# Attention with squared relu and an MLP behind it on one core: how the fourth and fifth head unit get transposed, and the order of the first loads

## The chip, the cores and the metric

The kernel runs on one core of one Trainium2 chip. The metric is the device time of one execution in microseconds (us); less is better. Before the change it is 379.6 us, the median of three runs (379.3 to 379.73).

## What is computed

```
scores = q @ k.T / sqrt(64)                  # 8 batches, 12 heads, 448 positions, head size 64
attn   = max(scores, 0)**2 / 448
x      = attn @ v                            # heads side by side: 3584 rows of 768
h      = x @ w_in                            # 768 -> 2048
out    = max(h, 0)**2 @ w_out                # 2048 -> 768
```

All inputs and the output are float32 in HBM; inside the kernel the operands are float16, which the loads make of them.

## The kernel before, in words

**Units and tiles.** Four heads of one batch are a *unit*: three units per batch, 24 in all, numbered 0 to 23. A unit has seven *tiles* (J = 7) of 64 key positions for each of its heads, so tile t belongs to unit t // 7; unit 4 begins with tile 28, unit 5 with 35, unit 6 with 42. For its scores a unit needs q and k with the head dimension on the partitions, that is transposed (`qT`, `kT`, from a pool of three buffers).

**Two ways to the transpose.** Units 0 to 5 (NPE = 6) are loaded by `load16` (lines 93 and 94: one DMA of 224 KB for q, one for k, in pieces of 896 B) and transposed on PE by `pe_transpose` (28 transposes into PSUM, line 222, and two copies out of it, lines 214 on ACT and 216 on DVE). Units 6 to 23 are loaded by `load_qk` (line 108: four DMAs of 112 KB, in pieces of 128 B, two for q and two for k) into `qs` and `ks`, and transposed by `dma_transpose`: two DMA transposes that SP issues (line 119), each after both halves of its source have landed. `load_v` (line 99) loads a unit's v, `load_w1` (line 134) a quarter of w_in in two DMAs, `load_w2` (line 140) a quarter of w_out.

**Queues.** All loads are issued by POOL, in the order of the program; at most eight are under way, since POOL waits for the eighth last before it issues the next. SP issues DMA transposes and stores. Each engine takes its instructions in the order in which the program writes them.

**The first part (up to about 26 us).** Batch 0, units 0 to 2, has nothing to lie beside: `visit` makes two tiles of scores (line 252, each twice, to keep PE busy), ACT applies the relu (line 256), DVE squares (line 369), and `av_some` multiplies attn with v (line 270) two visits later. PE transposes units 1, 2 and 3 in visits 1, 4 and 10.

**The h pass of batch 0 and 1 (about 28 to 84 us).** `h_group(b, f)` makes one block of 128 hidden units: six matmuls (line 420), relu on ACT or DVE, square on DVE. Between the blocks lies the attention of batch 1, units 3 to 5: an event list gives each piece of it a time on a clock that counts h matmuls (T_G = 6 x 0.1892 us a block, T_H = 16 blocks). `visit` now makes two tiles of scores, and `av_unit` a whole unit's attn x v (28 matmuls, line 317) once its seven tiles are there. In the second half of this pass, which belongs to batch 1, the events bring differences of w_out's quarters (`sums_w2`, DVE, line 151) and of w_in's (`sums_w1`), and the DMA transposes of units 6 and 7. Tile 42, the first of unit 6, comes at T_H + 8 T_G.

**The rest.** The out pass of batches 0 and 1 (line 729) and then, batch pair by batch pair, the h pass in a seven-product form (line 550) and the out pass, with the attention of the following pair between the blocks. What DVE may do late is kept in queues that a planner empties: it adds up the time of PE (`at_pe`) and of DVE (`at_ve`) from costs written in the code, 2.65 us for an `av_unit` and 0.19 + 0.38 per tile for a visit, and puts a piece of DVE work where it expects DVE to be free.

**PSUM.** Scores and transposes share the pool `slot` (two buffers of two banks, and a third one, `third`, up to its close). The h blocks' pool `mma` takes the banks of `third`; `mmb` those of the two pools of attn x v of batch 0 (`rounds`).

Around the change, the order of the first loads before it is:

```
load16(0); load_v(0); load16(1); load_v(1); load16(2); load_v(2)
# in visit 0: load16(3); load_w1(0); load_w1(1); load_v(3)
# in visit 2: load16(4); load_w1(2); load_v(4)
# in visit 5: load16(5); load_w1(3); load_v(5)
load_v(6); load_w2 (b11, b12, b22, b21); load_qk(6); load_qk(7)
```

Of the kernel before, what the change touches and what calls it, by code (L numbers as in the profile page):

```python
# [12 lines left out]
AF = mybir.ActivationFunctionType  # L13
# [4 lines left out]
def kernel(  # L18
# [9 lines left out]
    nc = tc.nc  # L28
# [13 lines left out]
    P = 128  # L42
    J = 7
# [4 lines left out]
    NF = FF // P  # L48
# [21 lines left out]
    PSUM = bass.MemoryType.PSUM  # L70
# [19 lines left out]
    def load16(n):  # L90
        tq = q16_p.tile([P, 2, J * D], FP16, name="q16", tag="q16")
        tk = q16_p.tile([P, 2, J * D], FP16, name="k16", tag="k16")
        nc.gpsimd.dma_start(out=tq, in_=heads(q, n))
        nc.gpsimd.dma_start(out=tk, in_=heads(k, n))
        q16s[n] = (tq, tk)

    def load_v(n):
        t = v_p.tile([P, 2, J * D], FP16, name="vt", tag="vt")
        nc.gpsimd.dma_start(out=t, in_=heads(v, n))
        vts[n] = t  # L100

    def load_qk(n):

        blks[n] = []
        for src, nm in ((q, "qs"), (k, "ks")):
            t = blk_p.tile([P, J, 2, D], FP16, name=nm, tag=nm)
            for hh in range(2):
                nc.gpsimd.dma_start(  # L108
                    out=t[:, :, hh, :],
                    in_=heads(src, n)[:, hh].rearrange("p (j d) -> p j d", d=D))  # L110
            blks[n].append(t)
# [20 lines left out]
    def load_w1(i):  # L132
        for hh in range(2):
            nc.gpsimd.dma_start(
                out=w1[i][64 * hh:64 * hh + 64],
                in_=moe_w_in[:, 512 * i:512 * (i + 1)].rearrange(
                    "(hh m d) f -> hh d m f", hh=2, d=D)[hh])
# [7 lines left out]
    def sums_w2(i):  # L145


        op, c = divmod(i, 2)
        c = slice(4 * c, 4 * c + 4)
        dst, x, y = ((t1, b12, b11), (t3, b22, b12), (t2, b22, t1), (nt4, b21, t2))[op]  # L150
        nc.vector.tensor_sub(dst[:, c], x[:, c], y[:, c])
# [5 lines left out]
    nc.vector.memset(zeros, 0.0)  # L157
    junk = const_p.tile([P, 1], FP16, name="junk", tag="junk")
    nc.scalar.activation(out=junk, in_=zeros[:, 0:1], func=AF.Relu)
    load_v(0)  # L160
    load16(1)
    load_v(1)
    load16(2)
    load_v(2)

    def sums_w1(i):

# [38 lines left out]
    def pe_transpose(n):  # L206
        srcs = q16s.pop(n)
        ts = new_qkt()
        ps = slot(FP16)

        def copy(i, eng):
            dst = ts[i].rearrange("p j c -> p (j c)")
            if eng == 0:
                nc.scalar.activation(out=dst, in_=pss[i][:, i, 0:J * P], func=AF.Copy)  # L214
            else:
                nc.vector.tensor_copy(dst, pss[i][:, i, 0:J * P])

        pss = [ps, slot(FP16) if n == 0 else ps]
        for i, src in enumerate(srcs):
            for j in range(J):  # L220
                for hh in range(2):
                    nc.tensor.transpose(  # L222
                        pss[i][64 * hh:64 * hh + 64, i, j * P:(j + 1) * P],
                        src[:, hh, j * D:(j + 1) * D], ident)
            if n == 0:
                copy(i, 1)
                warm(1)
        qkt[n] = ts
        if n == 3:
            return lambda: (copy(0, 0), copy(1, 0))  # L230
        if n > 0:
            copy(0, n < 3)
            copy(1, n < 3)
        return None


    xts: dict = {}
# [63 lines left out]
    def av_unit():  # L301

        n = unit[0]
        if n == NUN or seen.get(n * J + J - 1, 10 ** 6) >= now[0]:
            return
        unit[0] += 1
        flush(rest=False)
        at_pe[0] += 2.65
        b, u = divmod(n, NU)
        vt = vts[n]  # L310
        ps = slot(FP32)
        for j in range(J):
            at = ats.pop(n * J + j)
            for hp in range(2):
                r = slice(64 * hp, 64 * hp + 64)
                for hh in range(2):
                    nc.tensor.matmul(  # L317
                        ps[64 * hh:64 * hh + 64, hp, 0:S],
                        lhsT=vt[r, hh, j * D:(j + 1) * D], rhs=at[r, hh, :],
                        start=(j == 0), stop=(j == J - 1))  # L320
        if u == 0:
            xts[b] = x_p.tile([P, NM, S], FP16, name="xt", tag="xt")
        nc.scalar.activation(
            out=xts[b][:, 2 * u:2 * u + 2, :], in_=ps[:, :, 0:S],
            func=AF.Copy, scale=CX)
# [16 lines left out]
    at_pe = [0.0]  # L342
# [28 lines left out]
    def visit(tiles, turn=None, lag=2, most=3):  # L371
        now[0] += 1
        for t in tiles:
            if t % J == 0 and t >= NPE * J:
                prefetch(t // J + 2)
        if big:
            for t in tiles[:1]:
                score(t)
            av_unit()
            for t in tiles[1:]:  # L380
                score(t)
            at_pe[0] += 0.19 + 0.38 * len(tiles)
            for i, t in enumerate(tiles):
                square(ats[t], 0.6 + 0.85 * i)
            return
        for t in tiles:
            score(t, 2)
        later = pe_transpose(turn) if turn is not None else None
        flush()
        av_some(lag, most)  # L390
        if later:
            later()
        for t in tiles:
            square(ats[t])
        flush()
# [16 lines left out]
    def h_group(b, f):  # L412
        z = (b % 2) * S
        cell = [None]

        def step(m):
            def run():
                if m == 0:
                    cell[0] = mm_tile()
                nc.tensor.matmul(  # L420
                    cell[0][:, 0:S],
                    lhsT=w1[f // 4][:, m, (f % 4) * P:(f % 4 + 1) * P],
                    rhs=xts[b][:, m, :], start=(m == 0), stop=(m == NM - 1))
                if m < NM - 1:
                    return
                f0 = f - f % 2
                g = g_of(b)[:, f0:f0 + 2, z:z + S]
                if b == 0 and (f % 2 == 1 or f == 0) and f < 14:
                    nc.vector.tensor_scalar(
                        out=g[:, f % 2], in0=cell[0][:, 0:S],  # L430
                        scalar1=0.0, scalar2=None, op0=ALU.max)
                else:
                    nc.scalar.activation(
                        out=g[:, f % 2], in_=cell[0][:, 0:S], func=AF.Relu)
                flush()
                if b == 0 and f == NF - 1:
                    square(g)
                elif f % 2 == 1:
                    nc.vector.tensor_mul(g, g, g)
            return run  # L440

        return [(0.1892, step(m), m == 0) for m in range(NM)]
# [330 lines left out]
    NB0 = NU * J  # L773
    warm(10)
    pe_transpose(0)
    for i in range(11):
        visit([t for t in (2 * i, 2 * i + 1) if t < NB0],
              turn={1: 1, 4: 2, 10: 3}.get(i))
        if i == 0:
            load16(3)  # L780
            load_w1(0)
            load_w1(1)
            load_v(3)
        if i == 2:
            load16(4)
            load_w1(2)
            load_v(4)
        if i == 5:
            load16(5)
            load_w1(3)  # L790
            load_v(5)
    load_v(6)
    load_w2(b11, 0, 0)
    load_w2(b12, 0, 1)
# [2 lines left out]
    load_qk(6)  # L797
    load_qk(7)
    first.close()
    big.append(ctx.enter_context(tc.tile_pool(name="mma", bufs=2, space=PSUM)))  # L800


    f0 = h_group(0, 0)
    for _, fn, _ in f0[0:4]:
        fn()
    av_some(0, 9)
    rounds.close()
    big.append(ctx.enter_context(tc.tile_pool(
        name="mmb", bufs=2, space=PSUM, side="right", reuse_waits="tile")))
    visit([NB0, NB0 + 1])  # L810

    T_G = NM * 0.1892
# [3 lines left out]
    begin = [sum(T_O[:pr]) + 2 * (T_H + T_S * (pr - 1)) * (pr > 0) for pr in range(B // 2)]  # L816

    events = []
    seq = [[2, 3], 4, [4, 5], [6, 7], [8, 9], 5, [10, 11], [12, 13], [14, 15],
           [16, 17], [18, 19], [20], []]  # L820
    for i, ts in enumerate(seq):
        at = (2.5 + i) * T_G
        if isinstance(ts, int):
            events.append((at, lambda n=ts: pe_transpose(n)))
        else:
            events.append((at, lambda ts=ts: visit([NB0 + t for t in ts])))

    def ready():
        early.close()
# [3 lines left out]

    events.append((T_H + 0.2, ready))
    for i in range(8):
        events.append((T_H + (1 + i // 2) * T_G, lambda i=i: sums_w2(i)))
    for i in range(6):
        events.append((T_H + (8 + i) * T_G, lambda i=i: sums_w1(i)))
    for i in range(2):
        events.append((2 * T_H + 3 + 3 * i, lambda i=i: sums_w1(6 + i)))  # L840
    for m in (6, 7):
# [33 lines left out]
    for i in (1, 2):  # L875
        events.append((2 * T_H - (3 - i) * T_G, lambda i=i: outs[0][1](i)))

    steps = [(0.1892, None, False)] * 4 + f0[4:]
    for f in range(1, NF):
        steps += h_group(0, f)  # L880
    for f in range(NF):
        steps += h_group(1, f)
# [49 lines left out]
```

## Time and profile before

| what | us |
|---|---|
| median of three runs | 379.6 |
| the profiled execution, its own time | 379.35 |
| its span, first to last instruction | 377.6 |
| PE busy | 363.5 (96%) |
| DVE, ACT, POOL busy | 278.6, 249.8, 107.1 |
| PE idle from 0 to 8, 8 to 30 and 30 to 60.7 us | 1.7, 3.1, 1.1 |
| PE idle from 60.7 to 84.4 us | 0.0 |
| PE idle from 371 us to the end | 5.1 |
| one DMA transpose, from issue to landing (median) | 4.5 (qT), 4.2 (kT) |
| one load_qk half, one load_v, from issue to landing (median) | 4.4 to 5.3, 6.6 |

The page gives, for each engine, the busy time and its share of the span; then the span in 40 slices, with the busy share of each in tenths; the DMA queues (q0 is POOL's loads, q1 is SP's transposes and stores); and the groups of instructions by line, with tile names as out<-in. A wait is put down to what came last. The chain of waits is followed back from the last instruction, and the engine with most of it sets the end: here PE has 81%. The time from issue to landing of a DMA contains the time that it stands behind earlier ones in its queue.

### The profile page before, as it was taken

Reading aid. Unit: us, or ns where it says so; the run is one execution under the profiler, and the core shown is the slowest. Engines: PE = TensorE matmul, PEld = TensorE weight load, DVE = VectorE, ACT = ScalarE, POOL = GpSimd, SP = SyncE. Lnnn points to the kernel's source line nnn. Section 1 sums busy time; section 2 is a strip of 40 time slices with the busy share of each in tenths; the row PEclk is TensorE's granted clock in tenths of the full one; section 3 lists DMA queues with packets and bytes.
Section 4 is the critical chain, followed back from the end, with each engine's and each line's share of the span. In section 5 each row is a group of like instructions: output and inputs, shape, how many; then the busy total and the mean of one; then the engine's idle time right before and its main releaser. Section 6 shows DMA issues by size and latency. Waiting matters only on the chain.

```text
span 377.6 us, 8806 instructions
## 1 busy us (share of the span) xinstructions
PE 363.5 (96%) x3600; PEld 231.3 (61%) x3600; DVE 278.6 (74%) x515; ACT 249.8 (66%) x373; POOL 107.1 (28%) x128
## 2 busy tenths in 40 slices
PE   7889999999999999999999999999999999999994
PEld 3544444444455678785555577877555588985663
DVE  1796567997767689897965758989956688995542
ACT  2897996686677798775566578877766785532220
POOL 8545431944440444404042243150000000000001
PEclk9999999999999999999999999999999999999998
DMA  8999999999999999789498997893132200002333
GB/s 120 197 204 205 205 203 177 124 171 134 121 139 187 134 114 139 90 95 82 96 112 134 184 178 68 83 110 63 38 97 69 76 26 2 2 0 65 94 96 84
DMA packets 121160, 42.65 MB, mean 113 GB/s; under 512 B 100832, under 2 KB 117760, under 8 KB 121120
## 3 DMA queue, kind: packets, MB, share of 16 engines
q0 software_dynamic: 82912, 23.01, 59.9%
q1 hardware_dynamic: 38048, 18.98, 26.2%
q8 instruction: 28, 0.46, 0.5%
q10 hardware_dynamic: 160, 0.10, 0.1%
q14 instruction: 12, 0.10, 0.1%
HBM read 45.61 MB, written 11.01 MB: 150 GB/s over the span
## 4 chain that ended last, share of the span: by engine, by line
PE 81%; ACT 6%; DVE 6%; issue 2%; DMA 2%; POOL 1%; POOLq 0%; ACTq 0%; DVEq 0%
PE mm L729 33%; PE mm L550 23%; PE slot L252 9%; PE mm L420 9%; PE slot L317 7%; ACT at L256 4%; DVE at L369 2%; DMA k<-in_k_dram 2%; PE slot L222 1%; DVE g L491 1%; ACT m L486 1%; DVE xt L283 1%; DVE s L602 1%; DVE g L498 0%; ACT qT L214 0%
## 5 line engine op out<-in xcount | busy, mean ns | idle before, releaser
L256 ACT ACTIVATE at<-slot 128x896 f16<-128x896 f32 x168 | 146.2, 920 | 33.0 <-PE slot L252 33.0
L369 DVE TENSOR_TENSOR at<-at 128x896 f16<-128x896 f16 x168 | 99.7, 618 | 15.7 <-ACT at L256 14.5
L108 POOL DMA_DIRECT2D qs<-in_q_dram x36 | 35.4, 984 | 121.3 <-DMA qT<-qs 113.6
L729 PEld LDWEIGHTS <-s 128*128 128x128 f16 x440 | 41.7, 98 | 32.0 <-issue 4.3
L252 PE MATMUL slot<-qT,kT 64*64 64x448 f16 x756 | 58.1, 360 | 2.6 <-ACT at L256 1.2
L550 PEld LDWEIGHTS <-w 128*128 128x128 f16 x576 | 54.4, 98 | 5.9 <-issue 5.4
L550 PE MATMUL mm<-xt,w 128*128 128x224 f16 x432 | 48.6, 259 | 0.0
L729 PEld LDWEIGHTS <-g 128*128 128x128 f16 x336 | 31.5, 98 | 24.0 <-issue 5.0
L550 PEld LDWEIGHTS <-ws 128*128 128x128 f16 x432 | 40.2, 98 | 6.7 <-issue 6.7
L729 PE MATMUL mm<-b,g 128*128 128x384 f16 x224 | 40.7, 326 | 0.0
L420 PE MATMUL mm<-xt,w 128*128 128x448 f16 x192 | 39.6, 353 | 0.3 <-ACT xt L280 0.3
L729 PE MATMUL mm<-b,s 128*128 128x384 f16 x216 | 39.6, 326 | 0.1
L729 PE MATMUL mm<-t,s 128*128 128x384 f16 x224 | 39.5, 326 | 0.0
L636 DVE SCALAR_TENSOR_TENSOR osb<-mm,u 128x384 f32<-128x384 f32 (+1 forms) x30 | 16.2, 541 | 31.2 <-ACT u L631 23.0
L252 PEld LDWEIGHTS <-kT 64*64 64x64 f16 x756 | 19.9, 104 | 31.1 <-issue 25.7
L108 POOL DMA_DIRECT2D ks<-in_k_dram x36 | 35.0, 975 | 9.9 <-DMA b<-in_moe_w_out_dram 5.8
L631 ACT ACTIVATE u<-mm 128x384 f32<-128x384 f32 x28 | 13.7, 491 | 32.6 <-PE mm L729 31.4
L571 POOL DMA_DIRECT2D out_dram<-osb x2 | 1.1, 563 | 120.5 <-DVE osb L636 120.5
L550 PE MATMUL mm<-x,ws 128*128 128x224 f16 x288 | 34.4, 259 | 0.9 <-ACT m L486 0.9
L317 PE MATMUL slot<-at,vt 64*64 64x448 f16 x588 | 32.2, 350 | 0.6 <-DVE at L369 0.5
L498 DVE TENSOR_TENSOR g<-g 128x896 f16<-128x896 f16 x48 | 29.7, 619 | 1.1 <-ACT g L501 0.2
L420 PEld LDWEIGHTS <-w 128*128 128x128 f16 x192 | 17.3, 98 | 19.1 <-issue 4.8
(66 smaller groups left out, 400.2 us busy)
## 6 DMA issues: line engine op xcount, KB each, us to landing
out_dram<-osb SPq DMA_DIRECT2D x52, 192.0 KB, 3.3
vt<-in_v_dram POOLq DMA_DIRECT2D x24, 224.0 KB, 6.6
qs<-in_q_dram POOLq DMA_DIRECT2D x36, 112.0 KB, 4.4
ks<-in_k_dram POOLq DMA_DIRECT2D x36, 112.0 KB, 5.3
w<-in_moe_w_in_dram POOLq DMA_DIRECT2D x8, 384.0 KB, 11.5
b<-in_moe_w_out_dram POOLq DMA_DIRECT2D x4, 768.0 KB, 17.1
q<-in_q_dram POOLq DMA_DIRECT2D x6, 224.0 KB, 8.3
k<-in_k_dram POOLq DMA_DIRECT2D x6, 224.0 KB, 8.6
```

The lines of the kernel that those rows point to most:

```text
L108: nc.gpsimd.dma_start(out=t[:, :, hh, :], in_=heads(src, n)[:, hh].rearrange("p (j d) -> p j d", d=D))
L222: nc.tensor.transpose(pss[i][64 * hh:64 * hh + 64, i, j * P:(j + 1) * P], src[:, hh, j * D:(j + 1) * D], ident)
L252: nc.tensor.matmul(ps[c, hh, 0:S], lhsT=kT[r, j, c], rhs=qT[r, :, c], start=True, stop=True)
L256: nc.scalar.activation(out=at, in_=ps[:, :, 0:S], func=AF.Relu, scale=SK)
L317: nc.tensor.matmul(ps[64 * hh:64 * hh + 64, hp, 0:S], lhsT=vt[r, hh, j * D:(j + 1) * D], rhs=at[r, hh, :], start=(j == 0), stop=(j == J - 1))
L369: lambda: nc.vector.tensor_mul(at, at, at), 0))
L420: nc.tensor.matmul(cell[0][:, 0:S], lhsT=w1[f // 4][:, m, (f % 4) * P:(f % 4 + 1) * P], rhs=xts[b][:, m, :], start=(m == 0), stop=(m == NM ...
L498: due_g.append((t, 0.54, lambda: nc.vector.tensor_mul(g, g, g), b))
L550: nc.tensor.matmul(XY[s][y][:, r * Q:(r + 1) * Q], lhsT=left(k, i0 + 2 * s + r, m), rhs=right(k, m), start=(fresh and r == 0 and m == 0), ...
L631: nc.scalar.activation(out=t, in_=X[0][:, 0:HALF], func=AF.Copy, scale=CO)
L636: nc.vector.scalar_tensor_tensor(out=osb[row][:, c], in0=acc[0][:, 0:cc.stop - cc.start], scalar=CO, in1=keep[nm][:, cc], op0=ALU.mult, op ...
L729: nc.tensor.matmul(acc[0][:, 0:HALF], lhsT=left()[:, f], rhs=right[:, f], start=(fresh and f == 0), stop=(f == KH - 1), skip_group_check=n ...
```

## The change

Four things are changed.

- **Loads.** The q and k of units 1 and 2 are loaded ahead of the v of the unit before them. Unit 3 is loaded ahead of w_in. Units 4 and 5 are loaded by `load_qk`: unit 4 ahead of the first quarter of w_in, unit 5 ahead of v of unit 3 and the third quarter.
- **Transposes.** Units 4 and 5 go by `dma_transpose`, written after visit 6 and after the last visit of batch 0. `pe_transpose` of unit 3 comes after that visit's attn x v, and its kT is copied by DVE instead of ACT.
- **First h blocks.** Before, four matmuls of block 0 stood ahead of the last attn x v of batch 0. Now a part of attn x v stands ahead of the first two, and two more of block 0 and two of block 1 follow after the rest of it.
- **Events and costs.** The visits of batch 1 come every 1.33 blocks from 1.5 on. `sums_w2` and `sums_w1` come later. The planner's costs are 1.33 for an `av_unit` and 0.19 + 0.19 per tile for a visit.

PE loses 56 transposes and 56 weight loads by this, SP gains four DMA transposes; the bytes loaded are the same.

```diff
+    load16(1)
     load_v(0)
-    load16(1)
+    load16(2)
     load_v(1)
-    load16(2)
     load_v(2)
+    load16(3)
+    load_qk(4)
...
         if n == 3:
-            return lambda: (copy(0, 0), copy(1, 0))
+            return lambda: (copy(0, True), copy(1))
...
-        at_pe[0] += 2.65
+        at_pe[0] += 1.33
...
-            at_pe[0] += 0.19 + 0.38 * len(tiles)
+            at_pe[0] += 0.19 + 0.19 * len(tiles)
...
     for i in range(11):
-        visit([t for t in (2 * i, 2 * i + 1) if t < NB0],
-              turn={1: 1, 4: 2, 10: 3}.get(i))
+        visit([t for t in (2 * i, 2 * i + 1) if t < NB0], turn={1: 1, 4: 2}.get(i))
         if i == 0:
-            load16(3)
             load_w1(0)
             load_w1(1)
+        if i == 2:
+            load_qk(5)
             load_v(3)
-        if i == 2:
-            load16(4)
             load_w1(2)
             load_v(4)
         if i == 5:
-            load16(5)
             load_w1(3)
             load_v(5)
+        if i == 6:
+            dma_transpose(4)
+    later = pe_transpose(3)
+    dma_transpose(5)
     load_v(6)
...
-    big.append(ctx.enter_context(tc.tile_pool(name="mma", bufs=2, space=PSUM)))
-    f0 = h_group(0, 0)
-    for _, fn, _ in f0[0:4]:
-        fn()
+    big.append(ctx.enter_context(tc.tile_pool(
+        name="mma", bufs=2, space=PSUM, reuse_waits="tile")))
+    f0, f1 = h_group(0, 0), h_group(0, 1)
+    def some(part):
+        for _, fn, _ in part:
+            fn()
+    av_some(1, 9)
+    some(f0[0:2])
+    later()
     av_some(0, 9)
...
+    some(f0[2:4])
+    some(f1[0:2])
     visit([NB0, NB0 + 1])
...
-    seq = [[2, 3], 4, [4, 5], [6, 7], [8, 9], 5, [10, 11], [12, 13], [14, 15],
-           [16, 17], [18, 19], [20], []]
-    for i, ts in enumerate(seq):
-        at = (2.5 + i) * T_G
-        if isinstance(ts, int):
-            events.append((at, lambda n=ts: pe_transpose(n)))
-        else:
-            events.append((at, lambda ts=ts: visit([NB0 + t for t in ts])))
+    for i in range(11):
+        ts = [NB0 + t for t in (2 * i + 2, 2 * i + 3) if t < NB0]
+        events.append(((1.5 + 1.33 * i) * T_G, lambda ts=ts: visit(ts)))
...
     for i in range(8):
-        events.append((T_H + (1 + i // 2) * T_G, lambda i=i: sums_w2(i)))
+        events.append((T_H + (4 + 0.75 * i) * T_G, lambda i=i: sums_w2(i)))
     for i in range(6):
-        events.append((T_H + (8 + i) * T_G, lambda i=i: sums_w1(i)))
+        events.append((T_H + (10 + 0.8 * i) * T_G, lambda i=i: sums_w1(i)))
...
-    steps = [(0.1892, None, False)] * 4 + f0[4:]
-    for f in range(1, NF):
+    steps = [(0.1892, None, False)] * 6 + f1[2:4] + f0[4:6] + f1[4:6]
+    for f in range(2, NF):
```

## The prediction

> **What bounds the kernel now.** I read the page first (sections 1 and 2), then PE's waits up to 75 us, the chain of waits in order of time, SP's timeline, and last the DMA view stretch by stretch. TensorE (PE) is busy 96% of the span, so an edit pays only by taking PE work or PE waits away. PE's waits in the part that the change touches are few:
>
> ```profile
> PE slot L222 <- ACT at L256: 1.0, 3, 0.6
> PE slot L222 <- DMA k<-in_k_dram: 0.7, 1, 0.7
> PE avt L270 <- DVE xt L283: 0.7, 3, 0.4
> PE slot L252 <- ACT kT L214: 0.5, 2, 0.3
> ```
>
> The columns are total us, times, longest. The second line is k of unit 1 coming late; the fourth is the score blocks that wait for the PSUM copies of units 4 and 5. The chain shows the two PE transposes themselves, and the place where unit 6 is first used:
>
> ```profile
> 4.81 6.64 DMA k<-in_k_dram
> ...
> 34.78 0.92 PE slot L222 x28
> 35.72 0.92 ACT qT L214
> ...
> 44.25 0.92 PE slot L222 x28
> ...
> 60.80 10.32 PE mm L420 x54
> 71.12 0.50 PE slot L252 x8
> ```
>
> (start us, us). From 60.80 on PE runs without a gap, and at 71.12 it takes the first score tile of unit 6 (tile 42), the first unit that goes by DMA transposes. When these came is in SP's timeline:
>
> ```profile
> 59.98 1.31 SPq L119 DMA_TRANSPOSE qT<-qs  x1
> 61.55 1.23 SPq L119 DMA_TRANSPOSE kT<-ks  x1
> ```
>
> The second landed 4.4 us after its issue, at 61.55 + 4.4 = 65.95. SP issued it at once when the fourth load of unit 6 landed (issued on POOL at 42.95, 18.5 us to landing: 61.45). **So unit 6 has 71.12 - 65.95 = 5.17 us in hand, and that is all.** The last view is the DMA queues in four stretches (23 to 43 us; 57 to 61.5; 64 to 66; 72 to 81):
>
> ```profile
> DMA packets 4563, 4.09 MB, mean 204 GB/s; under 512 B 211, under 2 KB 4562, under 8 KB 4562
> ```
> ```profile
> DMA packets 5350, 0.70 MB, mean 156 GB/s; under 512 B 5308, under 2 KB 5350, under 8 KB 5350
> ```
> ```profile
> DMA packets 2176, 0.55 MB, mean 276 GB/s; under 512 B 2175, under 2 KB 2175, under 8 KB 2175
> ```
> ```profile
> q0 software_dynamic: 4397, 0.89, 123.0%
> q1 hardware_dynamic: 1856, 0.46, 52.0%
> ```
>
> The first is loads in the 896 B and 1 KB form (load16, load_v, load_w1): 204 GB/s. The second is load_qk's 128 B form alone: 156. The third is DMA transposes alone: 276. The fourth mixes loads (q0) and two transposes (q1). The DMA row of the page stands at 9 from the second slice to the sixteenth: from about 4 us until unit 6 and 7 have landed the loads leave no hole. There are thus two limits: PE, and 5 us behind it the DMA stream that ends with unit 6.
>
> [...]
>
> **The change part by part.** Sums are against the profiled execution: span 377.6 us, own time 379.35 (1.75 us around the span), 0.25 us under the median of 379.6.
>
> 1. k of unit 1 ahead of v0. The fourth load of the queue landed at 4.10 + 4.6 = 8.7 us, the fifth at 11.45. k1 becomes the fourth; its q is transposed at 10.20, held by ACT, so k no longer waits: -0.72 us. v0, now fifth, lands at about 11.45 and is first used at 12.79 - 0.72 = 12.07: hidden, 0.6 us to spare.
>
> 2. The last attn x v. Eight of its matmuls move ahead of unit 3's transposes and fill 0.50 of the 0.57 us in which these wait for ACT (at 26.57), and the four h matmuls that follow cover the copy to xt (0.25 us at 30.22, of which the rest of the new order keeps some): I take -0.55 us together. reuse_waits on the mma pool removes a wait that the trace doesn't show: 0.
>
> 3. Units 4 and 5 leave PE: 2 x 28 transposes, 2 x 0.92 us, and the two waits for their copies, 0.5: -2.35 us. ACT loses 2 x 2 copies of 0.92 us; it isn't late there, so nothing more. Visits of two tiles now come every 1.33 h blocks: 1.33 x 1.24 + 0.50 = 2.15 us of PE, with attn x v (1.32 us in 3.5 visits) 2.5; ACT's share is 2 x 0.92, a third of a 0.55 us relu or so, and 0.26 for attn x v's copy, 2.3 us. ACT keeps up, barely: 0, and 0.5 us if it doesn't.
>
> Sum on PE: -0.72 - 0.55 - 2.35 = **-3.6 us**, and tile 42 would be wanted at 71.12 - 3.6 = 67.5.
>
> 4. What the DMA stream gets. The same bytes stand ahead of unit 6 as before, but units 4 and 5 come as 128 B pieces: four loads of 114,688 B at 156 GB/s, 2.94 us a unit, for two of 229,376 B at 204, 2.25: +0.7 each, **+1.4 us**. Then four DMA transposes are put into the saturated stretch, on SP, which is idle there. What one takes from the loads is not shown for loads of this form, so I bound it. From its bytes: 229,376 B at 276 GB/s, 0.83 us. From the stretch 72 to 81 us: q0's 0.89 MB are 5.7 us of its work at 156 GB/s, so two transposes cost 3.3, 1.65 each; the worst single one (73 to 76 us: q0 moved 0.16 MB, 1.0 us of work) cost 2.0. Below 0.83 it goes if the engines work on both at once: from 104.5 to 107 us, with stores among it, they carried 247 GB/s; half the bytes' price, 0.4 us, is my lower end, an estimate. I take X = 1.5 us, near the mixed stretch: **+6.0 us**. Unit 6 thus lands 1.4 + 4X = 7.4 us later, at 73.35, if the way from load to landed transpose stays 4.5 us (the same loads of unit 7 are queued behind it in both).
>
> 5. On the way there. w1's first part (second half landed at 11.73 + 10.4 = 22.1 us) now stands behind unit 4: 22.1 + 2.94 = 25.0, and 1 to 2 transposes: 26.5 to 28, wanted at about 27.3. v3 was 27.1 and becomes 27.1 + 2 x 2.94 and two transposes, 35 to 37; wanted at about 37.3 (27.3 + 5.5 h blocks and three visits). w1's third part was 33.2; +1.4 + 4X = 40.6, wanted at about 42. Each may cost PE up to 1 us, but not in addition: time lost there makes unit 6 wanted later by the same. Unit 4 itself lands near 27 (wanted near 35.5), unit 5 near 41 (wanted near 43.6). w2's last part was at 36.87 + 21.2 = 58.1, now 65.5; its DVE differences are moved from 1 to 4 blocks after the first h pass to 4 to 9.25, so from about 64 on, that part at 69: hidden, and if not, DVE stalls in a stretch in which it has nothing to spare.
>
> 6. **Sum.** PE reaches tile 42 at 67.5 and waits until 73.35, in one piece or split with item 5. Behind that wait on PE stand all h blocks and the rest of the kernel, since PE takes its queue in order; from there on the kernel is as before. The end moves by 7.4 - 5.17 = **+2.2 us**: 379.35 + 2.2 = 381.6. Generally it moves by 1.4 + 4X - 5.17, but not under -3.6.
>
> 7. The planner's constants (at_pe 2.65 to 1.33, 0.38 to 0.19) reorder squares and relus on DVE from 126 us on; the instructions are the same. PE's waits in the passes at 151, 156, 221, 225, 238 and 253 us are 0.25 to 0.41 each, 1.8 together: between -1 and +1, I take 0. SP's later transposes and unit 7 to 9 shift with unit 6; unit 7 is wanted 8.6 us after it and landed 3 us after it: hidden.
>
> **The rivals.**
>
> [...]
>
> Rival B, the draw: a transpose costs its bytes alone, 0.83 us: 1.4 + 3.3 - 5.17 = -0.4, 378.9. For it: the 276 GB/s. Against: in every stretch with both queues at work the sum fell short of that.
>
> Rival C, faster: the engines carry transposes beside the loads. The place is the stream from 20 to 41 us, the price X; below X = 0.75 us the end moves by more than -0.76 us, at 0.4 us it is 1.4 + 1.6 - 5.17 = -2.2, 377.2, and at zero the whole 3.6 us of PE arrive, 375.8. For it: PE's saving is certain, and the large pieces of the loads may leave room that the 128 B pieces don't. Against: loads alone already hold the engines full.
>
> **How the numbers follow.** The measurement tells 0.2% (0.76 us) from no change. Forecast, X from 1.13 to 2.0 us, 380.1 to 383.2: 0.53. Rival A, above: 0.13. Within 0.2%, rival B and the edges of its neighbours: 0.15. Rival C: 0.19. That makes faster 0.19, same 0.15, slower 0.66. I predict 381.6. The range leaves out about a tenth on each side: 377.5 to 385.0; the likeliest case's own range is 380.1 to 383.2.
>
> **What would show it.** Right: PE's waits get an entry of several us at the scores, ended by a DMA (kT or qT), near 67 to 73 us; the last load of unit 6 lands at 66 to 70 instead of 61.45; PE transposes fall by 56 and the wait for k of unit 1 is gone. Wrong: no PE wait at tile 42 (then X is under 0.4, and the time under 377.5); waits at w1's parts that add up to more than unit 6 accounts for; or a change of the waits after 126 us by more than 1 us.

## The result, and the profile after

The changed kernel takes **389.4 us** (median of four runs, 387.8 to 391.2) against 379.45 us (378.8 to 379.7) before: a ratio of 1.0265, with a 95% interval of 1.0212 to 1.0318. It is slower, as forecast, but by 10.0 us and not by 2.2. The profiled execution is the longest of its four: own time 391.18 us, span 389.4 us, 11.8 us over the span of before. Lines moved by one or two: L253 is now the scores, L318 attn x v, L420 the h blocks, L370 DVE's square.

TensorE's waits in the profile after (total us, times, longest):

```profile
PE slot L253 <- DMA kT<-ks: 7.1, 2, 6.6
PE slot L318 <- DVE at L370: 5.1, 4, 3.0
...
PE slot L318 <- DMA vt<-in_v_dram: 0.6, 1, 0.6
```

Two large ones are new: a kT that comes from a DMA transpose, and DVE's squares. The timeline of PE shows where the first one stands (start us, us; in brackets the idle time before, and what ended it). Its first line is k of unit 1, which no longer comes late:

```profile
10.37 0.58 PE L224 MATMUL slot<-ident,k 128*64 128x128 f16 x14
...
36.04 0.38 PE L253 MATMUL slot<-qT,kT 64*64 64x448 f16 x4 [0.51 <-DMA kT<-ks]
...
38.62 1.52 PE L318 MATMUL slot<-at,vt 64*64 64x448 f16 x28 [0.64 <-DMA vt<-in_v_dram]
...
53.04 0.59 PE L253 MATMUL slot<-qT,kT 64*64 64x448 f16 x4 [6.57 <-DMA kT<-ks]
53.41 2.83 PE L318 MATMUL slot<-at,vt 64*64 64x448 f16 x28
...
56.55 2.22 PE L420 MATMUL mm<-xt,w 128*128 128x448 f16 x6
```

The 6.57 us are at the first tile of **unit 5**, not of unit 6. Behind them the 28 matmuls of an attn x v take 2.83 us instead of 1.52, and an h block 2.22 instead of 1.31. The same stretch by the microsecond says why; the column after the busy times is the granted clock, then the DMA share and GB/s:

```profile
52.00:53.00 1.00, 0.00 (x0) 0.00 (x0) 0.00 (x0) 0.00 (x0) 0.86 (x1) 0.50 1.33 200
53.00:54.00 1.00, 0.96 (x12) 0.62 (x16) 0.00 (x0) 0.33 (x1) 0.72 (x2) 0.50 1.32 205
```

TensorE's granted clock was 0.50. SP's timeline answers to the one shown of before; the first four lines are units 4 and 5, the last two unit 6:

```profile
20.61 2.05 SPq L119 DMA_TRANSPOSE qT<-qs  x1
23.32 3.65 SPq L119 DMA_TRANSPOSE kT<-ks  x1
36.06 1.22 SPq L119 DMA_TRANSPOSE qT<-qs  x1
37.58 4.33 SPq L119 DMA_TRANSPOSE kT<-ks  x1
71.04 1.22 SPq L119 DMA_TRANSPOSE qT<-qs  x1
72.62 1.23 SPq L119 DMA_TRANSPOSE kT<-ks  x1
```

From issue to landing the four of units 4 and 5 took 11.1, 12.7, 11.9 and 15.4 us (before, units 6 and 7: 4.1 to 5.1); those of unit 6 took 5.0 and 4.2. So kT of unit 5 landed at 37.58 + 15.4 = 53.0, where PE was waiting, and kT of unit 6 at 76.8. PE takes tile 42 at 76.89, without a wait, 5.8 us later than before (71.12). The last load of unit 6 landed about 72.6 where it had been 61.45: **11 us later**. No buffer held it back: in POOL's timeline the loads of unit 6 (from 48.53 us) are each released by the landing of an earlier load, and the buffers of unit 4 had been free since 36.0. The DMA view from 39 to 52.3 us, in which kT of unit 5 was under way:

```profile
DMA packets 3937, 2.42 MB, mean 182 GB/s; under 512 B 1950, under 2 KB 3935, under 8 KB 3935
...
q0 software_dynamic: 2086, 1.93, 92.6%
q1 hardware_dynamic: 1849, 0.46, 32.2%
...
kT<-ks SPq DMA_TRANSPOSE x1, 15.4
```

(queue: pieces, MB, share.) Loads (q0) and transposes (q1) went nearly one piece for one here (2086 to 1849), and q1's pieces are some 250 B (0.46 MB / 1849).

After tile 42 the rest of the loss comes in two places, both at attn x v waiting for DVE. The first, in the timeline of PE:

```profile
88.62 1.30 PE L318 MATMUL slot<-at,vt 64*64 64x448 f16 x24
92.88 0.59 PE L318 MATMUL slot<-at,vt 64*64 64x448 f16 x4 [2.96 <-DVE at L370]
...
93.77 3.84 PE L729 MATMUL mm<-b,g 128*128 128x384 f16 x16
```

2.96 us, and a granted clock of 0.50 again behind it, to 95.97 us (at 98.05 us, with the clock back at 1.00, 16 matmuls of line 729 take 2.77 us). The second is 1.64 us at 285.7 us. The span adds up: 5.8 at tile 42, 2.96 + 1.64, and about 1.5 of slow clock after the 2.96: 11.9 of 11.8 us.

### The profile page after: what moved, and what is told of

Read it like the earlier page. It is cut to its first block, busy times and chain, and to the rows that moved or that the text cites. A ratio compares the mean times of both kernels' runs of the same rounds, so it can differ in the third digit from the quotient of the medians.

```text
span 389.4 us, 8698 instructions
## 1 busy us (share of the span) xinstructions
PE 364.6 (94%) x3544; PEld 230.2 (59%) x3544; DVE 279.5 (72%) x516; ACT 245.9 (63%) x368; POOL 111.5 (29%) x132
## 4 chain that ended last, share of the span: by engine, by line
PE 66%; DMA 12%; DVE 12%; ACT 5%; issue 3%; POOL 1%; POOLq 0%; ACTq 0%; DVEq 0%
PE mm L729 30%; PE mm L550 22%; PE slot L253 7%; PE slot L318 5%; DMA b<-in_moe_w_out_dram 5%; ACT at L257 4%; DVE at L370 3%; DMA kT<-ks 3%; DMA qs<-in_q_dram 3%; DVE s L602 1%; DMA k<-in_k_dram 1%; DVE g L498 1%; DVE t L151 1%; ACT m L486 1%; DVE g L491 1%
## 5 line engine op out<-in xcount | busy, mean ns | idle before, releaser
L370 DVE TENSOR_TENSOR at<-at 128x896 f16<-128x896 f16 x168 | 100.2, 619 | 26.2 <-ACT at L257 24.8
L108 POOL DMA_DIRECT2D qs<-in_q_dram x40 | 39.3, 984 | 123.3 <-DMA qT<-qs 113.8
L253 PE MATMUL slot<-qT,kT 64*64 64x448 f16 x756 | 58.6, 364 | 9.1 <-DMA kT<-ks 7.1
L550 PEld LDWEIGHTS <-w 128*128 128x128 f16 x576 | 54.4, 98 | 5.9 <-issue 5.4
L108 POOL DMA_DIRECT2D ks<-in_k_dram x40 | 38.6, 967 | 12.9 <-DMA b<-in_moe_w_out_dram 6.3
L729 PE MATMUL mm<-b,g 128*128 128x384 f16 x224 | 41.8, 332 | 0.0
L253 PEld LDWEIGHTS <-kT 64*64 64x64 f16 x756 | 19.7, 105 | 37.4 <-issue 24.6
L420 PE MATMUL mm<-xt,w 128*128 128x448 f16 x192 | 40.4, 359 | 0.0
L318 PE MATMUL slot<-at,vt 64*64 64x448 f16 x588 | 34.0, 363 | 5.8 <-DVE at L370 5.1
L324 ACT ACTIVATE xt<-slot 128x896 f16<-128x896 f32 x21 | 19.3, 917 | 17.1 <-PE slot L318 17.1
```

The lines of the kernel that those rows point to most:

```text
L108: nc.gpsimd.dma_start(out=t[:, :, hh, :], in_=heads(src, n)[:, hh].rearrange("p (j d) -> p j d", d=D))
L253: nc.tensor.matmul(ps[c, hh, 0:S], lhsT=kT[r, j, c], rhs=qT[r, :, c], start=True, stop=True)
L318: nc.tensor.matmul(ps[64 * hh:64 * hh + 64, hp, 0:S], lhsT=vt[r, hh, j * D:(j + 1) * D], rhs=at[r, hh, :], start=(j == 0), stop=(j == J - 1))
L324: nc.scalar.activation(out=xts[b][:, 2 * u:2 * u + 2, :], in_=ps[:, :, 0:S], func=AF.Copy, scale=CX)
L370: lambda: nc.vector.tensor_mul(at, at, at), 0))
L420: nc.tensor.matmul(cell[0][:, 0:S], lhsT=w1[f // 4][:, m, (f % 4) * P:(f % 4 + 1) * P], rhs=xts[b][:, m, :], start=(m == 0), stop=(m == NM ...
```

## The experiments

All are set against the kernel before, on the same chip, as a ratio. Four questions were open: is unit 5 late because its transposes are slow or because its loads are; what makes a transpose slow; what do the two waits for DVE come from; and what does each part of the change cost by itself.

### Units 4 and 5 transposed on PE from the same tiles

```
 # after, with these lines:
-            dma_transpose(4)           -    dma_transpose(5)
+    for n, i in ((4, 2), (5, 6)):
+        events.append(((0.84 + 1.33 * i) * T_G, lambda n=n: pe_transpose(n)))
 # pe_transpose reads blks[n] as src[:, j, hh, :]; its two copies go to ACT
```

> The changed kernel with units 4 and 5 loaded as it loads them (128 B pieces, same place in the queue), but transposed on PE out of these tiles, with the copies on ACT, two thirds of an h block ahead of their first scores. No DMA transpose of units 4 and 5 is left. Theory 1 (a DMA transpose amid large loads takes 11 to 15 us from issue to landing, and starves the loads behind it): the 6.6 us wait at tile 35 and the 0.5 us wait at tile 28 are gone, so is the half clock after them (2.6 us); PE gets 2 x 0.92 us of transposes and some 0.4 us of waits for their copies back. From 389.4: 389.4 - 9.7 - 0.6 + 2.3 = about 381.5. Rival 2 (the loads of units 4 and 5 come late in any case, by their form and their place): PE waits at the transposes of unit 5 for its last load, 3 us or more, and the time stays over 385.

Measured: 384.9 us, ratio 1.0151 (1.0125 to 1.0176). The waits for kT and the half clock at 53 us are gone, and PE waits for no load of unit 4 or 5, so their loads were in time and their transposes were not. The time is above what was expected. The copies on ACT brought waits of 0.94 us ahead of unit 5's transposes and 0.57 us behind them, where 0.4 had been allowed for; and the sum took waits of the profiled execution (391.2 us) from the median (389.4). Both waits for DVE, which the sum had left in, are still there (2.98 and 1.65 us).

### The sums at their old times

```
-    events.append((T_H + (4 + 0.75 * i) * T_G, lambda i=i: sums_w2(i)))
+    events.append((T_H + (1 + i // 2) * T_G, lambda i=i: sums_w2(i)))
-    events.append((T_H + (10 + 0.8 * i) * T_G, lambda i=i: sums_w1(i)))
+    events.append((T_H + (8 + i) * T_G, lambda i=i: sums_w1(i)))
```

> The changed kernel with the DVE differences of w_out and w_in at their old times (1 to 4 blocks into the second h pass, and 8 to 13). Theory (DVE is full in this stretch, and what is put 3 to 5 blocks later there comes out at the end as a wait of attn x v for squares): the 3.0 us wait at 92.9 us and the slow clock after it, 1.1 to 1.5 us, are gone: about 385. Rival (DVE is late since w_out itself is late): DVE waits for w_out's quarters at the old times, and the wait at the end of the pass stays, 389.

Measured: 385.9 us, ratio 1.0182 (1.0156 to 1.0207), by the ratios 3.1 us less than the changed kernel. PE's waits in this run:

```profile
PE slot L253 <- DMA kT<-ks: 7.4, 2, 6.2
PE slot L318 <- DVE at L370: 2.2, 3, 1.6
```

The wait of 2.96 us is gone; the loads of w2, on which the sums depend, are nearly as late as in the changed kernel (the last one is issued at 45.07 instead of 46.06 us; before, at 36.87), and in the profile after DVE takes its first difference at 73.56 us without waiting for a load. So it was not late data: the new due times put the sums into DVE's queue where it has no idle time left (73.6 to 95 us in the profile after). The second wait for kT is 1.19 us at tile 42: unit 6 is now the later one.

### The planner's costs as before

```
-        at_pe[0] += 1.33
+        at_pe[0] += 2.65
-            at_pe[0] += 0.19 + 0.19 * len(tiles)
+            at_pe[0] += 0.19 + 0.38 * len(tiles)
```

> The changed kernel with the planner's old costs (2.65; 0.19 + 0.38 per tile). Theory (the new costs put squares and relus into another order on DVE, which makes attn x v wait 1.64 us at 285.7 us): that wait is gone, 389.4 - 1.6 = 387.8. Rival (the wait is a late result of what happened before 95 us): it stays, 389.4.

Measured: 387.9 us, ratio 1.023 (1.0183 to 1.0277). By the ratios that is 1.3 us less than the changed kernel, but the intervals of the two ratios overlap; what is sure is the trace, in which the wait at 285.7 us is gone, as expected, and nothing new came:

```profile
PE slot L253 <- DMA kT<-ks: 6.5, 1, 6.5
PE slot L318 <- DVE at L370: 3.5, 3, 3.0
```

### Transposes and loads by themselves

```
for n, (bulk, count) in enumerate(((None, 0), (bulk_896, 24), (None, 0),
                                   (bulk_768, 8), (None, 0), (bulk_128, 40), (None, 0))):
    load_qk(n)
    dma_transpose(n)
    for i in range(count):
        bulk(i)          # v of a unit, a quarter of w_out, half of v in 128 B pieces
```

> A measurement alone: attention and MLP are left out and the output is zeros. Pairs of DMA transposes of one unit are issued as its loads land, first with nothing behind them, then behind each pair a row of loads: 24 of 224 KB in 896 B pieces, 8 of 768 KB in 768 B pieces, 40 of 112 KB in 128 B pieces, with an idle stretch between the rows. Theory 1: alone a transpose lands 3 to 5 us after its issue; amid large pieces 11 to 15 us, with the loads at about three quarters of their rate meanwhile; amid 128 B pieces something between, with the loads at less than half their rate. Rival (the long way in the changed kernel came from what else ran there): 4 to 7 us in each row.

Measured: alone, a transpose lands 2.9 to 3.3 us after its issue. Amid loads of v (896 B pieces) qT takes 9.2 and kT 12.4 us; amid quarters of w_out 10.5 and 13.1. The row meant for 128 B pieces missed its aim: source and target were both contiguous, and the pieces came out at 896 B (7.3 and 9.2 us). The DMA view amid w_out, from 66 to 72 us, and then, from 74 to 90, of the loads alone:

```profile
DMA packets 2277, 1.14 MB, mean 191 GB/s; under 512 B 1157, under 2 KB 2277, under 8 KB 2277
...
q0 software_dynamic: 1139, 0.86, 91.3%
q1 hardware_dynamic: 1138, 0.28, 36.3%
```
```profile
DMA packets 4303, 3.26 MB, mean 204 GB/s; under 512 B 66, under 2 KB 4302, under 8 KB 4302
```

1139 pieces to 1138: **one for one** in this stretch. A load's piece there is some 755 B on average (0.86 MB / 1139), a transpose's some 250 B, so the transposes get 0.28 MB in 6 us, 47 GB/s, and the loads fall from 204 to 143. A transpose has 229,376 B; at 47 GB/s that is 4.9 us, and the two of a unit share the queue: 9.8 us of flow for the pair.

The row that had missed was made again, with targets that force the 128 B pieces:

```
t = small_p.tile([P, J, 2, D], FP16, ...)
for hh in range(2):
    nc.gpsimd.dma_start(out=t[:, :, hh, :], in_=heads(v, n)[:, hh].rearrange("p (j d) -> p j d", d=D))
```

> Loads and transposes alone, no arithmetic (the output is zeros): the two transposes of a unit are issued into a queue of 16 loads in 896-byte pieces, then into one of 16 loads cut into pieces of 128 bytes, which the earlier measurement had meant to do and did not. Theory (shares go by packets, so the size of the loads' pieces sets a transpose's share): amid 896 bytes they land 9 and 12 us after issue as before, amid 128 bytes in 4 to 7, as those of unit 6 and 7 do in the kernel before. Rival (the short way in the kernel before came from a queue that was running empty, not from the piece size): amid a full queue of 128-byte pieces they take 9 us or more too.

Measured: amid 896 B pieces 10.5 and 13.5 us, amid 128 B pieces 6.2 and 6.8. In both rows loads stood in the queue all the while (they took 7.7 and 6.2 us to landing). The DMA view in the second, from 50 to 56 us:

```profile
DMA packets 5237, 0.88 MB, mean 147 GB/s; under 512 B 5237, under 2 KB 5237, under 8 KB 5237
...
q0 software_dynamic: 3471, 0.44, 132.4%
q1 hardware_dynamic: 1766, 0.44, 59.8%
```

Here the pieces go two for one and the bytes half and half: the transposes get 73 GB/s, 3.1 us each. So loads in the queue were not enough to make the way long, as the rival had it: it was long beside 896 B pieces (10.5 and 13.5 us) and short beside 128 B ones (6.2 and 6.8). The transposes got a quarter of the bytes beside the large pieces of w_out (0.28 of 1.14 MB) and half beside the 128 B ones (0.44 of 0.88 MB). Two for one is no rule, though. In the changed kernel, from 29 to 32 us, most loads have small pieces too (1310 of all 1357 pieces are under 512 B), and the pieces go one for one, at 104 GB/s in all; why is open:

```profile
q1 hardware_dynamic: 680, 0.17, 98.0%
q0 software_dynamic: 676, 0.13, 71.4%
```

### The parts of the change, one upon the other

The first has the order of the loads alone, the second also the first h blocks around the last attn x v, with units 4 and 5 as before on PE.

```
 # before, with:  load16(1); load_v(0); load16(2); load_v(1); load_v(2)
```

> The kernel before, with one thing of the change: k and q of unit 1 are loaded ahead of v of unit 0, and unit 2 ahead of v of unit 1. Theory: the 0.7 us that PE waits for k of unit 1 go, v of unit 0 still comes in time, and as PE has no gap from there to the end of the h passes, all 0.7 us arrive: about 378.7 us where the kernel before takes 379.4. Rival: v of unit 0 is late instead and the first attn x v waits as long: no change.

Measured: 378.3 us, ratio 0.9978 (0.9969 to 0.9988). As expected: -0.8 us.

```
 # the same, with unit 3 out of visit 10, and after the loop:
+    later = pe_transpose(3)
 ...
+    f0, f1 = h_group(0, 0), h_group(0, 1)
+    av_some(1, 9); some(f0[0:2]); later(); av_some(0, 9)
 ...
+    some(f0[2:4]); some(f1[0:2])
     visit([NB0, NB0 + 1])
```

> The kernel before with the load order and with the first h blocks around the last attn x v of unit 0 to 3 (unit 3 transposed after attn x v, one copy on DVE, the reused waits of the mma pool); units 4 and 5 are transposed on PE, the sums and the planner's costs are those of before. Theory: -0.7 for the order and about -0.6 for the layout: 378.0 to 378.2. Rival: the layout only moves its waits to the next group: the same as the order alone, 378.7.

Measured: 377.8 us, ratio 0.9966 (0.9953 to 0.9979): another -0.45 us. The two intervals overlap, but the times were taken on the same chip and their means are 0.44 us apart, each with a standard deviation of 0.2. This is the fastest kernel of the study, 0.34% under the kernel before.

The next has all of the change but its due times and planner's costs, so that the DMA transposes of units 4 and 5 are in it:

```
 # after, with the edits of "The sums at their old times" and "The planner's costs as before"
```

> The changed kernel with the old due times of the sums and the old costs of the planner: of the change remain the load order, the layout and the DMA transposes of units 4 and 5. Theory: the wait for the sums at 92.9 us (2.96) and the one at 285.7 us (1.64) go, the long wait for k of unit 5 stays; since the sums alone brought 3.5 us and the planner's costs 1.4, the time is about 384.4. Set against the kernel with order and layout alone it prices the DMA transposes of units 4 and 5 at about +6 us net of the PE work that they save. Rival: the two gains overlap, and the wait for unit 6 (1.2 us with the old sums) grows: 386.

Measured: 384.3 us, ratio 1.0133 (1.0110 to 1.0155), as expected: the two gains add up (the planner's costs are worth 1.9 us here, against the run with the old due times alone), and it is 6.4 us over the kernel with order and layout. That still holds more than the transposes. Its counterpart has them on PE:

```
 # the same, with units 4 and 5 on PE from blks, as in the first experiment
```

> The changed kernel with units 4 and 5 transposed on PE from their tiles in 128-byte pieces, with the old due times of the sums and the old costs of the planner: of the change remain the order, the layout and the form of the loads of units 4 and 5. Theory: the three faults (long way of the transposes, sums late, planner's order) account for all of the loss, so this is the kernel with order and layout (377.8) plus the PE waits of its copies on ACT (0.9 and 0.6): 379.3, and not over 379.6; each load form costs unit 6 some 3.4 us of its 5.2 in hand, so it does not wait. Rival: the form alone makes unit 6 late: a wait at tile 42 of a kT, 380 or more.

Measured: 379.0 us, ratio 1.0006 (1.0000 to 1.0013), and no wait for a kT. The timeline of PE in the two of them, first with DMA transposes, then without:

```profile
51.94 0.59 PE L253 MATMUL slot<-qT,kT 64*64 64x448 f16 x4 [6.70 <-DMA kT<-ks]
...
76.03 0.57 PE L253 MATMUL slot<-qT,kT 64*64 64x448 f16 x8 [1.00 <-DMA kT<-ks]
```
```profile
46.41 0.58 PE L229 MATMUL slot<-ident,qs 128*64 128x128 f16 x14 [0.94 <-ACT at L262]
...
49.20 0.38 PE L258 MATMUL slot<-qT,kT 64*64 64x448 f16 x4 [0.57 <-ACT kT L221]
...
70.72 0.57 PE L258 MATMUL slot<-qT,kT 64*64 64x448 f16 x8
```

The last line of each is tile 42. SP could issue the transposes of unit 6 at 70.22 and 71.80 with them and at 61.77 and 63.35 without: both 8.45 us apart. **Four DMA transposes in the loaded stretch cost the stream 8.45 us, 2.1 each**, and the 128 B form alone 1.8 (61.77 against 59.98 before). These are single executions. The other such pair, the changed kernel (71.04) and the first experiment (63.49), has 7.55 between them, 1.9 each; and the first experiment, with the same loads as the run without transposes here, is itself 1.7 us later than that one, so the form alone is less sure than the transposes.

The change as a sum of the ratios' differences, at 379 us:

| step | ratio | adds, us |
|---|---|---|
| order of the loads | 0.9978 | -0.8 |
| first h blocks | 0.9966 | -0.45 |
| units 4 and 5 in 128 B form, still on PE, copies on ACT, new spacing | 1.0006 | +1.5 |
| their transposes by DMA | 1.0133 | +4.8 |
| due times of the sums, planner's costs | 1.0265 | +5.0 |

The +1.5 is as much as the two waits for ACT in the run of the third row (0.94 and 0.57), which the changed kernel hasn't got; no wait in that run is for a load or a transpose of unit 4, 5 or 6. So what the form, the spacing and the DMA transposes cost the changed kernel is the third and the fourth row together, some 6.3 us. The last row does not need the transposes: the first experiment and the run of the third row, both without them, differ in the due times and costs alone and are 5.5 us apart (1.0151 and 1.0006).

### Unit 4 alone, with time in hand

```
 # the kernel with order and layout, with:
     load_v(2)
+    load_qk(4)              # and no load16(4), no pe_transpose(4)
 ...
+        if i == 4:
+            dma_transpose(4)
 ...
+    load_qk(6)              # moved ahead of the last two load_w2
     load_w2(b22, 1, 1); load_w2(b21, 1, 0)
```

> As the kernel with order and layout, but unit 4 alone leaves PE: it is loaded in 128-byte pieces and transposed by DMA, and its two transposes are issued some 15 us ahead of its first score instead of 5; unit 5 stays on PE; unit 6 is loaded before the last parts of w2. Theory (lag): given 11 to 13 us from issue to landing, they land near 32, 3 us ahead of use, so nothing waits for them, and 28 PE transposes and their wait go: 1.0 to 1.2 us less, about 377.0. Rival (share): wherever they are put, they take their 1.9 to 2.8 us each from the loads, so something loaded there (v or the first weights) comes late: a new PE wait of 1 us or more beside a DMA, 378 or more.

Measured: 380.15 us, ratio 1.0029 (1.0013 to 1.0044). The timeline of PE:

```profile
69.59 0.57 PE L253 MATMUL slot<-qT,kT 64*64 64x448 f16 x8 [0.71 <-DMA kT<-ks]
...
80.61 0.59 PE L253 MATMUL slot<-qT,kT 64*64 64x448 f16 x4 [2.00 <-DMA kT<-ks]
81.13 3.83 PE L421 MATMUL mm<-xt,w 128*128 128x448 f16 x12
```

Unit 4 was in time, with nothing to spare: its kT took 16.3 us from 19.13 and landed at 35.4, where PE needed it. PE was 0.6 us ahead of the kernel with order and layout at tile 42 (68.88 against 69.46), and then waited for units 6 and 7, and ran at a granted clock of 0.50 behind the second wait: 12 h matmuls in 3.83 us for 2.44. Neither theory named these two waits. The profiled execution took 381.6 us, 1.4 over the median, so they need not be as long in every one. As unit 6 had been moved ahead of w_out's last quarters, its transposes flew amid large pieces (10.2 and 11.2 us to landing), so the edit had two things in it. Unit 7's kT took 8.9 us. The next run takes the move back:

```
     load_w2(b22, 1, 1); load_w2(b21, 1, 0)
+    load_qk(6)
```

> As the kernel with order, layout and unit 4 alone by DMA transposes, with unit 6 loaded behind w2 again, as in the kernel before. Lag theory: the two waits of that kernel (0.7 us at the first tile of unit 6, 2.0 at one of unit 7) came because moving unit 6 ahead put its transposes amid the large pieces of w2, 10 us from issue to landing; with it behind w2 they are issued amid 128-byte pieces and land in 5: unit 6 is loaded some 5 us later than in the kernel before (66 to 67), transposed by 71.5, wanted at 68.9: one wait of about 2.5 us, the wait at unit 7 gone: 377.8 - 0.6 + 2.5 = 379.7. Share rival: the same bytes and turns, so the same time as before the move: 380.1 with the waits only moved, and half clock behind them.

Measured: 378.7 us, ratio 1.0003 (0.9994 to 1.0011), better than either theory said. One wait:

```profile
70.45 0.57 PE L253 MATMUL slot<-qT,kT 64*64 64x448 f16 x8 [1.44 <-DMA kT<-ks]
```

Unit 6's kT was issued at 66.08 instead of 61.77 in the kernel with order and layout (4.3 us for one unit's form and two transposes). Unit 6's transposes landed in 5.1 and 4.3 us, beside 128 B pieces, and unit 7's in 3.6 and 3.0, with hardly a load beside them. The kernel loses 0.9 us to the one with order and layout alone (1.4 by the ratios, which were taken on two chips): -0.6 of PE work, +1.44 of waiting.

A last run tried to get that wait back by loading v of unit 6 behind unit 7:

```
-    load_v(6)
 ...
     load_qk(7)
+    load_v(6)
```

> As the last kernel with unit 4 alone by DMA transposes, with v of unit 6 loaded behind unit 7 instead of ahead of w2: 229,376 bytes less stand ahead of unit 6, 1.1 us at 204 GB/s. Theory (unit 6's time is a sum of the bytes and transposes ahead of it): unit 6 is transposed 1.1 us sooner, so the wait of 1.44 us at tile 42 shrinks to 0.3 and the time falls by 1.1 us from 378.7 to 377.6, about what order and layout alone give or a little less. Rival (something else holds unit 6, such as the buffers that its loads wait for): no change, 378.7.

Measured: 378.8 us, ratio 1.0005 (0.9997 to 1.0013): no gain. The wait shrank only from 1.44 to 1.13 us, and not because unit 6 came sooner: its kT was issued 0.6 us sooner, but took 5.5 us instead of 4.3 and landed at 71.0 instead of 70.4. PE reached tile 42 0.9 us later, 0.5 of it by a wait for k of unit 5 that the run before had not. Unit 4's qT was issued 0.9 us later too, so the stream itself may have gained the 1.1 us; this execution does not settle it.

## Why the prediction was right or wrong

The direction was right, and for the reason given: the kernel with the order, the layout and the DMA transposes alone is 5.0 us slower, since unit 6 comes late. Of the miss of 7.8 us, 2.8 are step 4, which priced a transpose and the form too low. The other 5.0 are two terms that the prediction put at nothing: the sums of step 5 and the planner's costs of step 7.

**Step 1, order of the loads: right.** -0.72 said, -0.8 measured. No profiled execution with this order waits for k of unit 1. Waits of 0.2 to 0.7 us for q, in seven of the eleven, are for unit 0: PE begins its transposes at 5.1 to 5.2 us with either order.

**Step 2, layout: right.** -0.55 said, -0.45 measured.

**Step 3, PE's saving: right, and larger in the changed kernel.** The waits up to tile 42 and the half clock come to 7.7 + 2.6 = 10.3 us there, and tile 42 is 5.8 late, so some 4.5 us had been saved where 3.6 were said.

**Step 4, the price of a transpose: the first term that failed, in size.** X = 1.5 was chosen, with bounds of 0.4 and 2.0; it is 1.9 to 2.1, and the form is 1.8 instead of 1.4. The mechanism, "it moves by 1.4 + 4X - 5.17", holds: 1.8 + 8.45 - 5.17 = +5.1, and the kernel that has this and not the due times is 5.0 us slower than before. What X lacked was not what a transpose takes from the loads. In the measurements without arithmetic the loads lose 1.5 us to a transpose amid large pieces (204 to 143 GB/s for 4.9 us) and 1.6 amid 128 B pieces (155 GB/s from 60 to 66 us, without transposes, to 73 for 3.1 us): the way was longer amid large pieces (10.5 and 13.1 us against 6.2 and 6.8), the price was not. Some 2.3 of the 8.45 us went in two stretches in which the queues moved little, an estimate worked out in the last section; their cause is open. (The sum has a slip as well: X = 2.0 gives 379.35 + 4.23 = 383.6, not the 383.2 of the range.)

**Step 5, the way there: wrong in place.** "Unit 4 itself lands near 27 (wanted near 35.5), unit 5 near 41 (wanted near 43.6)." The loads were where it put them; the transposes were not, since the 4.5 us from issue to landing, taken beside 128 B pieces, were 11 to 15. Unit 4 came at 36.0 and unit 5 at 53.0, so PE stood 6.57 us at unit 5. What this adds at tile 42 is little, though: unit 6, landing at 76.8, would have held PE there. With the old due times unit 6 made PE wait a further 1.0 to 1.2 us behind unit 5's wait. The waits are not additive, as step 5 said. That is argued from the traces: no run removed unit 5's wait and kept all four transposes; the run with unit 4 alone shows the wait at unit 6 without any at units 4 and 5. v of unit 3 cost 0.64 us, within the 1 us allowed.

**Step 5, the sums: the second failure.** "hidden, and if not, DVE stalls in a stretch in which it has nothing to spare". The second half was the case, and it had been given no price. Not the data was late, as that step feared: the due times moved the work into the full stretch. By their ratios the due times alone are 3.1 us; in the trace they are 2.96 of wait and 1.5 of slow clock, against which the run without them has 1.19 more at tile 42.

**Step 7, the planner's costs: third.** 0 was taken between -1 and +1; the trace has +1.64, the ratios 1.3 against the changed kernel and 1.9 against the run with the old due times. Together with the sums this is 5.0 us, about two thirds of the miss.

**Rival A, with 0.13 above the forecast,** was a price for a lower clock behind a wait at tile 42. No run of before shows such a price (the mean granted clock there is 0.997); it was the author's estimate. What the runs showed stood at other places: a granted clock of 0.50 after the wait of 6.57 us at unit 5, worth 2.6 us, and after the 2.96 us, worth about 1.5, where nothing absorbs it. **Rivals B and C** needed X at 0.83 or below; four transposes measured together, at 1.9 to 2.1 each, exclude that.

**Its signs.** "No PE wait at tile 42" was to mean X under 0.4. It came, and meant something else: PE had stood at unit 5 and reached tile 42 just as unit 6 landed. The last load of unit 6 (72.6, where 66 to 70 was said) and the new wait after 126 us told the truth.

## What to carry to other kernels

A DMA transpose put beside saturated loads has to be priced in that stretch: here its way was 10.5 and 13.5 us beside 896 B pieces and 6.2 and 6.8 beside 128 B ones, and what the transposes took was paid by the last in the stream, unit 6, which nobody had touched (its last load 11 us later). Do not take the time from issue to landing from another stretch without looking at the pieces that fly there. An edit of due times or planner's costs is a change of its own: look for an engine without idle time in the stretch it moves work into, and give "if not hidden" a price.

## What was not expected of the hardware

**Half clock behind four waits.** PE's granted clock fell to 0.50 behind the wait of 2.00 us in the run with unit 4 and unit 6 moved, those of 2.96 and 6.57 in the profile after, and that of 6.70 in the kernel with the old due times and costs; behind those of 1.00, 1.19, 1.44 and 1.64 us it stood at 1.00. In the run with unit 4 and unit 6 moved, by the microsecond:

```profile
80.00:81.00 1.00, 0.39 (x4) 0.13 (x4) 1.00 (x2) 0.00 (x0) 0.02 (x1) 0.79 1.76 217
81.00:82.00 1.00, 1.00 (x7) 0.43 (x4) 0.64 (x2) 0.75 (x1) 0.90 (x1) 0.50 1.68 222
...
83.00:84.00 1.00, 1.00 (x4) 0.43 (x3) 0.43 (x1) 0.41 (x1) 1.00 (x3) 0.51 1.89 113
```

The clock fell at about 80.6, 2.0 us after PE's last work, and was back at 84: 3.4 us at half speed, 1.4 us lost in the h blocks (3.83 for 2.44). In the profile after it was at 0.50 from 92.56 to 95.97 us, 3.41 us, and from 51.60 to 58.43, 6.83 us; it fell there 2.6 and 5.1 us after PE's last work. In the kernel with the old due times and costs it was at 0.50 from 50 to 54 us and at 0.68, on average, from 54 to 56. What sets the moment of the fall and its length was not shown.

**A hole in the DMA stream.** In the profile after, all queues together moved about 10 GB/s from 32.5 to 33.5 us and 19 from 43.5 to 44, while transposes were under way and loads were queued. The kernel with the same loads and no transposes there shows no such hole: from 28 to 46 us none of 40 slices is under 156 GB/s. Two of the kernels with unit 4 alone by DMA transposes, which move some 200 GB/s around it, fall to 99 and 90 and to 107 and 125 GB/s from 30 to 32 us. In the kernel with the old due times and costs:

```profile
29.00:33.00 4.00, 3.92 (x30) 1.63 (x31) 3.07 (x6) 3.98 (x6) 1.02 (x2) 1.00 1.78 88
42.45:43.25 0.80, 0.80 (x6) 0.32 (x4) 0.80 (x2) 0.28 (x1) 0.40 (x1) 1.00 0.33 17
```

At the 147 GB/s measured beside 128 B pieces the first stretch's bytes would have taken 2.4 us of its 4, so 1.6 are lost there, and some 0.7 in the second: 2.3 us, an estimate. What stops the engines was not settled.
